# Row transfers between HBM and SBUF cut into four groups of 32 partitions instead of two halves of 128

## The chip, the cores and the metric

The kernel runs on one core of a Trainium2 chip. The metric is the device time of one execution in microseconds (us). The kernel before takes 1252.09 us (median of 2 runs, 1251.47 to 1252.70).

## The reference, cut to what matters

Forward and backward pass of one transformer block on x of 2048 rows by 512 columns, bfloat16. The attention is local and dilated: with 32 heads of 16 columns, row s looks at the rows s, s-2, ..., s-14. The block is followed by a GELU feed-forward layer of 1792 columns. Outputs are the block's result (out_0), the gradient of x (out_1) and those of the six weights and biases.

```python
H = 32; W, dil = 8, 2
idx = pos[:, None] - (jnp.arange(W) * dil)[None, :]
logits = jnp.einsum("bhsd,bhswd->bhsw", q, k[idx]) * Dh ** -0.5   # masked where idx < 0
o = jnp.einsum("bhsw,bhswd->bhsd", _softmax(logits), v[idx])
h = x + o @ wo                                  # x @ wqkv on _layernorm(x) gave q, k, v
out = h + (_gelu(_layernorm(h) @ w1 + b1) @ w2 + b2)
_out, _vjp = jax.vjp(_f, A_x, A_wqkv, A_wo, B_w1, B_b1, B_w2, B_b2)
```

## The kernel before

The 2048 rows are worked on in four chunks (c = 0 to 3). A chunk does not hold 512 neighbouring rows: 32 places of 64 rows each are formed (`TPR` = 64, `PR` = 32), and chunk c takes 16 neighbouring rows out of each place. A tile of a chunk, [128, 4, 512], holds them so: partition 32 n + p, for n = 0 to 3, has of place p the rows 2n, 2n+1 of the first eight and the same two of the last eight. So a chunk is moved between such a tile and a plain array in HBM by an access pattern of three dimensions: 4 (the n), 32 (the p), two rows in a piece.

Three helpers do this. `put_rows` (L152) writes a tile to HBM and `get_rows` (L156) reads one, each in two halves of 128 partitions through `half_rows` (L147), whose outermost dimension is `Q4` = 4. `row4` (L226) reads whole rows for the weighted sums: a tile of 128 partitions by 10 rows of 1 KB, in two pieces of five rows; here too the outermost dimension on the HBM side is 4, since the four groups of 32 partitions start one window step apart. `feat4` (L248) and `att4` (L238) read parts of rows, and already in four groups of 32 partitions.

```python
return _ap(ap2d, [[2 * n, Q4], [TPR * n, PR], [1, 2 * n]], off=(pad + CJ * c + HJ * f) * n)   # half_rows
in_=_ap(d_t[:, :], [[abs(shift) * n, Q4], [TPR * n, PR], [1, nn * n]], off=(t0 + j0) * n)     # row4
```

The program has these stages; times are of the profiled execution.

- Forward, 0 to about 430 us. `f_qkv` (L290) normalises a chunk, forms q, k and v with TensorE, copies them from PSUM to SBUF with ScalarE (`qkv`, L304) and writes them with `put_rows` from POOL to `k_r`, `q_r`, `v_r`. `f_attn` (L307) reads parts of rows back (`k`, `q`), forms logits and softmax and writes the weights (`at_r`). `f_o` (L331) reads rows of `v_r` with `row4` and sums them (`wsum`, L272: VectorE multiplies at L279, TensorE adds up at L285). `f_h` adds x, read anew with `get_rows`. `f_ffn` (L362) is the feed-forward layer; it writes out_0 in halves from the ACT queue (L397).
- First part of backward, about 430 to 690 us: the feed-forward layer's gradients. `gout` is read with `get_rows` from POOL (L459). Here TensorE is busy nearly all the time.
- Second part of backward, about 690 to 1185 us: attention. `b_go` (L591) writes `go_r` with `put_rows`; `b_ga` (L603) reads `bv` and `go` with `feat4`, VectorE multiplies (L262), and `gl_r` is written; `b_sum` (L620) runs three times per chunk (sel 2, 0, 1), each time with two `row4` tiles `r` (of `go_r`, `k_r`, `q_r`; pool tag `w4`, three buffers) and eight multiplications at L279; `b_gx` (L641) forms the gradient of x (`ln_bwd`, last step `gx`, L489) and writes out_1 in halves from POOL (L657). In between, `weights_gen` (L665) puts in the products for the weights' gradients, with tiles `h1tm` of 1 MB.
- Last, to 1247 us: the gradient of wqkv (L734) from tiles read again.

The order on each engine is made by the tile scheduler that builds the program: it lists the instructions of each queue by its own estimate of when they can start, and each queue then runs in that order. DMAs are issued by SP (`sync`), ACT and POOL (`pq`); a queue's next DMA waits behind one whose data are not ready. Each DMA has one of eight completion semaphores of its kind (one set for SP and ACT, one for POOL), used in turn, so that a ninth DMA waits for the first.

Of the kernel before, what the change touches and what calls it, by code (L numbers as in the profile page):

```python
# [10 lines left out]
P = 128  # L11
BF16 = mybir.dt.bfloat16
# [14 lines left out]
Q4 = 4  # L27
PR = P // Q4


def _ap(a, dims, off=0):
    return bass.AP(tensor=a.tensor, offset=a.offset + off, ap=[list(d) for d in dims])
# [3 lines left out]
def kernel(  # L36
# [20 lines left out]
    nc = tc.nc  # L57
    xf = A_x.flatten_outer_dims()
    gof = grad_out.flatten_outer_dims()
    out0f = out_0.flatten_outer_dims()  # L60
# [83 lines left out]
    def pv(d_t):  # L144
        return d_t[:, :].rearrange("p (t d) -> p t d", t=TC)

    def half_rows(ap2d, c, f, pad=0):  # L147

        n = ap2d.shape[-1]
        return _ap(ap2d, [[2 * n, Q4], [TPR * n, PR], [1, 2 * n]], off=(pad + CJ * c + HJ * f) * n)  # L150

    def put_rows(eng, ap2d, c, t_, pad=0):  # L152
        for f in range(2):
            eng.dma_start(out=half_rows(ap2d, c, f, pad), in_=t_[:, 2 * f:2 * f + 2, :].rearrange("p i d -> p (i d)"))

    def get_rows(eng, t_, ap2d, c):  # L156
        for f in range(2):
            eng.dma_start(out=t_[:, 2 * f:2 * f + 2, :].rearrange("p i d -> p (i d)"), in_=half_rows(ap2d, c, f))


    fl = pool("fl", 1)
# [64 lines left out]
    def row4(pool_, d_t, t0, nj, name, tag, bufs, shift):  # L226


        n = d_t.shape[-1]
        t_ = pool_.tile([P, nj, n], BF16, name=name, tag=tag, bufs=bufs)  # L230
        t0 += min(0, shift) * (Q4 - 1)
        for j0 in range(0, nj, 5):
            nn = min(5, nj - j0)
            sync.dma_start(out=t_[:, j0:j0 + nn, :],  # L234
                           in_=_ap(d_t[:, :], [[abs(shift) * n, Q4], [TPR * n, PR], [1, nn * n]], off=(t0 + j0) * n))
        return t_

    def att4(pool_, d_t, t0, nj, name, tag, bufs, shift):  # L238
# [123 lines left out]
    def f_ffn(c):  # L362
        h, ln2T = hs[c], l2T[c]
        gs = []
        for f2 in range(FT // 2):
            u = fl.tile([P, 2, CH], BF16, name=f"u{c}_{f2}", tag="u", bufs=3)
            for i in range(2):
                ft = 2 * f2 + i
                ps = acc(f"psf{c}_{ft}", "accB")
                for dc in range(DC):  # L370
                    nc.tensor.matmul(ps[:], lhsT=w1[:, dc, ft * P:(ft + 1) * P], rhs=ln2T[:, dc, :],  # L371
                                     start=(dc == 0), stop=(dc == DC - 1))
                nc.scalar.activation(out=u[:, i, :], in_=ps[:], func=ACT.Identity, bias=b1c[:, ft:ft + 1], scale=1.0)  # L373
            z = fl.tile([P, 2, CH], BF16, name=f"z{c}_{f2}", tag="z", bufs=2)
            nc.vector.tensor_tensor(out=z[:], in0=u[:], in1=u[:], op=ALU.mult)
            nc.vector.tensor_scalar(out=z[:], in0=z[:], scalar1=GK, scalar2=1.0, op0=ALU.mult, op1=ALU.add)
            nc.vector.tensor_tensor(out=z[:], in0=z[:], in1=u[:], op=ALU.mult)
            s = fl.tile([P, 2, CH], BF16, name=f"s{c}_{f2}", tag="s", bufs=2)
            nc.scalar.activation(out=s[:], in_=z[:], func=ACT.Sigmoid, scale=2.0 * GC)
            gt = fl.tile([P, 2, CH], BF16, name=f"g{c}_{f2}", tag="g", bufs=7)  # L380
            nc.vector.tensor_tensor(out=gt[:], in0=u[:], in1=s[:], op=ALU.mult)
            gs.append(gt)
            r0, r1 = 2 * f2 * P, (2 * f2 + 2) * P
            for dd, t_ in ((x_d[c][r0:r1, :], u), (s_d[c][r0:r1, :], s), (g_d[r0:r1, c * CH:(c + 1) * CH], gt)):
                pq.dma_start(out=dd.rearrange("(i p) t -> p i t", p=P), in_=t_[:])
        for j in range(TC):
            ps = acc(f"ps2{c}_{j}", "accB")
            for ft in range(FT):
                nc.tensor.matmul(ps[:], lhsT=gs[ft // 2][:, ft % 2, j * P:(j + 1) * P], rhs=w2[:, ft, :],  # L389
                                 start=(ft == 0), stop=False)  # L390
            nc.tensor.matmul(ps[:], lhsT=ones_row[:], rhs=b2row[:], start=False, stop=False)
            nc.tensor.matmul(ps[:], lhsT=ident[:], rhs=h[:, j, :], start=False, stop=True)
            if j % 2 == 0:
                o0 = fl.tile([P, 2, D], BF16, name=f"o0{c}_{j}", tag="o0", bufs=2)
            nc.scalar.copy(out=o0[:, j % 2, :], in_=ps[:])
            if j % 2 == 1:
                nc.scalar.dma_start(out=half_rows(out0f, c, j // 2), in_=o0[:].rearrange("p i d -> p (i d)"))  # L397

    def f_wT(src, ns, dst, nb):
        n2 = 8 // ns if ns <= 8 else 1  # L400
# [76 lines left out]
    def ln_bwd(ps, xhat, r, resid, out_ap, nm):  # L477
        s2 = const.tile([P, 2], F32, name=f"s2{nm}", tag="s2", bufs=4)
        junk = bl.tile([P, D], BF16, name=f"jk{nm}", tag="junk", bufs=2)
        nc.scalar.activation(out=junk[:], in_=ps, func=ACT.Identity, accum_out=s2[:, 0:1])  # L480
        junk2 = bl.tile([P, D], BF16, name=f"jl{nm}", tag="junk", bufs=2)
        nc.vector.tensor_tensor_reduce(out=junk2[:], in0=ps, in1=xhat, scale=1.0, scalar=0.0,
                                       op0=ALU.mult, op1=ALU.add, accum_out=s2[:, 1:2])
        c2 = const.tile([P, 2], F32, name=f"c2{nm}", tag="c2", bufs=4)
        nc.vector.tensor_scalar(out=c2[:], in0=s2[:], scalar1=r, scalar2=-1.0 / D, op0=ALU.mult, op1=ALU.mult)
        u = bl.tile([P, D], F32, name=f"lu{nm}", tag="lu", bufs=2)
        nc.scalar.activation(out=u[:], in_=xhat, func=ACT.Identity, bias=c2[:, 0:1], scale=c2[:, 1:2])
        nc.vector.scalar_tensor_tensor(out=u[:], in0=ps, scalar=r, in1=u[:], op0=ALU.mult, op1=ALU.add)  # L488
        nc.vector.tensor_tensor(out=out_ap, in0=u[:], in1=resid, op=ALU.add)  # L489
# [151 lines left out]
    def b_gx(c):  # L641
        ln1 = bp.tile([P, TC, D], BF16, name=f"bln1{c}", tag="bln1", bufs=1)
        pq.dma_start(out=ln1[:], in_=pv(ln1_d[c]))
        for j in range(TC):
            ps = acc(f"psy{c}_{j}", "gx", 2)
            n = 0
            for sel in (2, 0, 1):
                for g in range(G):
                    nc.tensor.matmul(ps[:], lhsT=gts[c, sel][:, g, j * P:(j + 1) * P], rhs=wqkvT[:, sel * G + g, :],  # L649
                                     start=(n == 0), stop=(n == NJ - 1))  # L650
                    n += 1
            t = c * TC + j
            if j % 2 == 0:
                gx = bp.tile([P, 2, D], BF16, name=f"gx{t}", tag="gx", bufs=2)
            ln_bwd(ps[:], ln1[:, j, :], rstd1[:, t:t + 1], gh[c][:, j, :], gx[:, j % 2, :], f"a{t}")
            if j % 2 == 1:
                pq.dma_start(out=half_rows(out1f, c, j // 2), in_=gx[:].rearrange("p i d -> p (i d)"))  # L657

    br1.release()
    bp = pool("bp", 1, side="right")  # L660
# [111 lines left out]
```

## Time and profile before

| what | us |
|---|---|
| median of 2 runs | 1252.09 (1251.47 to 1252.70) |
| the profiled execution | 1248.67 |
| its span, first to last instruction | 1246.9 |
| busy in the span: TensorE, VectorE, ScalarE, POOL | 756.1, 560.1, 436.6, 331.8 |
| mean granted clock of TensorE | 0.795 of full |

An engine's busy time is the sum over its instructions. A wait is put down to the instruction or DMA that came last before the waiting engine could go on. The chain is followed back from the last instruction, at each step to what released it. The DMA share is the mean busy share of the 16 DMA engines.

### The profile page before, as it was taken

To read this page: it belongs to the slowest core of one execution; us is meant where nothing else is said; L and a number is where in the kernel's file an instruction comes from. 1 tells how busy PE (TensorE), PEld (TensorE's weight loads), DVE (VectorE), ACT (ScalarE), POOL (GpSimd) and SP (SyncE) were. 2 spreads that over 40 slices of the span, in tenths; PEclk is the share of its full clock that TensorE was granted. 3 is DMA by queue.
4 is the path that set the end of the run, shared out by engine and by line. 5 is a ranking of instruction groups with operands and counts; after the bars stand their busy time and mean duration, and the time that the engine had idled before them with its cause. 6 is when DMAs were issued, how large, how long until landed. Compare 5 with 4: busy or idle time off the path is not lost.

```text
span 1246.9 us, 11658 instructions
## 1 busy us (share of the span) xinstructions
PE 756.1 (61%) x4306; PEld 343.9 (28%) x4306; DVE 560.1 (45%) x879; ACT 436.6 (35%) x600; POOL 331.8 (27%) x474
## 2 busy tenths in 40 slices
PE   1664515656558859999998626443445354454558
PEld 0322102322223324444454314120113122121123
DVE  3210355660855544888763034618346253253400
ACT  2333203543344545878775301020220221121201
POOL 3333222442242744443220323132032111100020
PEclk9887756687879989999999859575667776787669
DMA  6555434465354896666552776463365554433071
GB/s 200 157 131 141 113 72 125 156 195 157 108 187 154 273 279 200 191 186 180 174 154 89 194 154 148 133 158 104 117 174 147 148 157 138 139 131 124 30 291 38
DMA packets 72006, 191.54 MB, mean 154 GB/s; under 512 B 19821, under 2 KB 27854, under 8 KB 71950
## 3 DMA queue, kind: packets, MB, share of 16 engines
q0 software_dynamic: 49920, 128.67, 37.2%
q1 hardware_dynamic: 12892, 54.27, 12.5%
q10 hardware_dynamic: 9138, 7.87, 2.1%
q8 instruction: 33, 0.54, 0.2%
q14 instruction: 23, 0.19, 0.1%
HBM read 122.43 MB, written 68.24 MB: 153 GB/s over the span
## 4 chain that ended last, share of the span: by engine, by line
DMA 34%; issue 20%; PE 19%; DVE 11%; POOL 7%; ACT 5%; another core or an unknown queue 2%; SPq 2%; ACTq 0%; POOLq 0%; DVEq 0%
DMA r<-go_r 6%; DMA h1tm<-h1tm_d 4%; DMA k_r<-qkv 4%; PE psq L734 4%; DMA r<-q_r 3%; DMA r<-k_r 2%; DVE pb L279 2%; PE psw L677 2%; PE ps L389 2%; DMA s_d<-s 2%; DMA gout<-in_grad_out_dram 2%; SPq L234 2%; DMA w1T_d<-wT 2%; PE psw L509 1%
## 5 line engine op out<-in xcount | busy, mean ns | idle before, releaser
L279 DVE TENSOR_TENSOR pb<-ba,r 128x2048 bf16<-128x2048 bf16 x96 | 113.4, 1220 | 149.1 <-DMA r<-go_r 68.4
L285 PE MATMUL pss<-pb,sel 128*32 128x512 bf16 x384 | 48.1, 497 | 123.6 <-DVE pb L279 122.9
L262 DVE TENSOR_TENSOR pag<-go,bv 128x4096 bf16<-128x4096 bf16 x16 | 36.3, 2288 | 121.0 <-DMA go<-go_r 98.1
L649 PE MATMUL psy<-wqkvT,gT 128*128 128x512 bf16 x192 | 65.4, 491 | 29.4 <-ACT gT L224 18.9
L302 PE MATMUL psq<-wqkv,ln1T 128*128 128x512 bf16 x192 | 59.2, 466 | 39.2 <-ACT qkv L304 38.3
L371 PE MATMUL psf<-ln2T,w 128*128 128x512 bf16 x224 | 66.2, 441 | 25.1 <-ACT u L373 25.1
L677 PE MATMUL psw<-h1tm,ln2a 128*128 128x256 bf16 x448 | 65.7, 298 | 24.7 <-DMA h1tm<-h1tm_d 22.1
L637 ACT ACTIVATE gt<-pss 128x512 bf16<-128x512 f32 x32 | 19.0, 598 | 143.2 <-PE pss L285 141.7
L262 DVE TENSOR_TENSOR pa<-q,k 128x4096 bf16<-128x4096 bf16 x16 | 36.3, 2287 | 69.9 <-DMA k_r<-qkv 48.5
L285 PEld LDWEIGHTS <-sel 128*32 128x32 bf16 x512 | 15.2, 97 | 182.6 <-issue 100.4
L389 PE MATMUL ps<-w,g 128*128 128x512 bf16 x224 | 56.7, 400 | 3.9 <-ACT u L373 3.1
L544 PE MATMUL psg<-goutT,w2T 128*128 128x512 bf16 x224 | 58.0, 379 | 0.1
L677 PEld LDWEIGHTS <-ln2a 128*128 128x128 bf16 x448 | 44.2, 105 | 46.1 <-issue 21.0
L734 PE MATMUL psq<-gqa,ln1a 128*128 128x512 bf16 x192 | 44.1, 395 | 19.3 <-DMA gqa<-gq_d 19.3
L509 PE MATMUL psw<-gout,gtm 128*128 128x512 bf16 x224 | 53.0, 379 | 0.0
L565 PE MATMUL psx<-w1T,gh 128*128 128x512 bf16 x224 | 52.1, 379 | 1.2 <-DVE luf L488 1.1
L304 ACT CAST qkv<-psq 128x512 bf16<-128x512 f32 x48 | 27.2, 588 | 62.9 <-DMA k_r<-qkv 34.6
L279 DVE TENSOR_TENSOR pbo<-a,v 128x2048 bf16<-128x2048 bf16 x32 | 38.0, 1216 | 22.7 <-PE pso L285 21.1
L268 PE MATMUL ga<-pag,sel 128*32 128x512 bf16 x128 | 17.3, 562 | 48.9 <-DVE pag L262 48.9
L638 POOL DMA_DIRECT2D gq_d<-gt x12 | 6.9, 575 | 146.9 <-ACT gt L637 79.5
L373 ACT ACTIVATE u<-psf,b1c 128x512 bf16<-128x512 f32 x56 | 36.8, 686 | 21.3 <-DMA x_d<-u 10.9
L546 DVE CUSTOM_DVE_ANT_0 gh<-psg,by 128x512 bf16<-128x512 f32 x56 | 37.6, 687 | 13.6 <-PE psg L544 12.7
(191 smaller groups left out, 1573.9 us busy)
## 6 DMA issues: line engine op xcount, KB each, us to landing
v<-v_r SPq DMA_DIRECT2D x16, 640.0 KB
r<-go_r SPq DMA_DIRECT2D x16, 640.0 KB
r<-k_r SPq DMA_DIRECT2D x16, 640.0 KB
r<-q_r SPq DMA_DIRECT2D x16, 640.0 KB
x_d<-u POOLq DMA_DIRECT2D x28, 256.0 KB, 4.6
s_d<-s POOLq DMA_DIRECT2D x28, 256.0 KB, 4.1
g_d<-g POOLq DMA_DIRECT2D x28, 256.0 KB, 4.7
bu<-x_d POOLq DMA_DIRECT2D x28, 256.0 KB, 3.6
```

Source lines behind the costliest of these rows:

```text
L262: nc.vector.tensor_tensor(out=pr[:], in0=_ap(q_ap, [q_ap.ap[0], [P, 4], [0, W], [1, P]]), in1=_ap(k_ap, [k_ap.ap[0], [P, 4], [-DIL * P, W] ...
L279: nc.vector.tensor_tensor(out=pr[:].rearrange("p n (d h) -> p n d h", h=H), in0=_ap(a_ap, [a_ap.ap[0], [4 * H, 4], [0, DH], [1, H]], off=w ...
L285: nc.tensor.matmul(ps[PR * n:PR * n + PR, :], lhsT=sel4[:], rhs=prs[wh][:, n, :], start=(wh == 0), stop=(wh == 1))
L302: nc.tensor.matmul(ps[:], lhsT=ln1T[:, dc, j * P:(j + 1) * P], rhs=wqkv[:, dc, sel * D:(sel + 1) * D], start=(dc == 0), stop=(dc == DC - 1))
L371: nc.tensor.matmul(ps[:], lhsT=w1[:, dc, ft * P:(ft + 1) * P], rhs=ln2T[:, dc, :], start=(dc == 0), stop=(dc == DC - 1))
L389: nc.tensor.matmul(ps[:], lhsT=gs[ft // 2][:, ft % 2, j * P:(j + 1) * P], rhs=w2[:, ft, :], start=(ft == 0), stop=False)
L509: nc.tensor.matmul(ps[:], lhsT=gtm[:, t, :], rhs=gout[t // TC][:, t % TC, :], start=(t == 0), stop=(t == NT - 1))
L544: nc.tensor.matmul(ps[:], lhsT=w2T[:, dc, ft * P:(ft + 1) * P], rhs=gT[:, dc, :], start=(dc == 0), stop=(dc == DC - 1))
L565: nc.tensor.matmul(ps[:], lhsT=gh1[ft // 2][:, ft % 2, j * P:(j + 1) * P], rhs=w1T[:, ft, :], start=(ft == 0), stop=(ft == FT - 1))
L649: nc.tensor.matmul(ps[:], lhsT=gts[c, sel][:, g, j * P:(j + 1) * P], rhs=wqkvT[:, sel * G + g, :], start=(n == 0), stop=(n == NJ - 1))
L677: nc.tensor.matmul(ps[:, i * 2 * P:(i + 1) * 2 * P], lhsT=ln2a[:, t // TC, t % TC, dc * P:(dc + 1) * P], rhs=tmx[:, t, :], start=(t == 0), ...
L734: nc.tensor.matmul(ps[:], lhsT=ln1a[:, t // TC, t % TC, dc * P:(dc + 1) * P], rhs=gqt[:, t // TC, t % TC, :], start=(t == NT - 1), stop=(t ...
```

## The change

`half_rows` goes. `rows` describes one group n of 32 partitions: 32 places outermost, then the two pairs of rows. `put_rows` and `get_rows` issue four such DMAs for a tile (256 KB halves become 128 KB quarters for a [128, 4, 512] tile) where there were two. `row4` issues four DMAs, one for each group of 32 partitions with all its 10 rows, where there were two of 128 partitions by five rows. out_0 and out_1 are now gathered in a tile of the whole chunk with one buffer (before: two buffers of half a chunk) and written at the chunk's end with `put_rows` from SP; before, out_0 was written from ACT and out_1 from POOL.

```diff
-        return _ap(ap2d, [[2 * n, Q4], [TPR * n, PR], [1, 2 * n]], off=(pad + CJ * c + HJ * f) * n)
+    def rows(ap2d, c, n, pad=0):
+        m = ap2d.shape[-1]
+        return _ap(ap2d, [[TPR * m, PR], [HJ * m, 2], [1, 2 * m]], off=(pad + CJ * c + 2 * n) * m)
+
+    def quarter(t_, n):
+        return t_[PR * n:PR * n + PR, :, :].rearrange("p (f i) d -> p f (i d)", f=2)
 
     def put_rows(eng, ap2d, c, t_, pad=0):
-        for f in range(2):
-            eng.dma_start(out=half_rows(ap2d, c, f, pad), in_=t_[:, 2 * f:2 * f + 2, :].rearrange("p i d -> p (i d)"))
+        for n in range(Q4):
+            eng.dma_start(out=rows(ap2d, c, n, pad), in_=quarter(t_, n))
...
@@ row4
-        for j0 in range(0, nj, 5):
-            nn = min(5, nj - j0)
-            sync.dma_start(out=t_[:, j0:j0 + nn, :],
-                           in_=_ap(d_t[:, :], [[abs(shift) * n, Q4], [TPR * n, PR], [1, nn * n]], off=(t0 + j0) * n))
+        for s_ in range(Q4):
+            sync.dma_start(out=t_[PR * s_:PR * s_ + PR, :, :].rearrange("p (a b) d -> p a (b d)", a=2),
+                           in_=_ap(d_t[:, :], [[TPR * n, PR], [nj // 2 * n, 2], [1, nj // 2 * n]], off=(t0 + abs(shift) * s_) * n))
@@ f_ffn
-            if j % 2 == 0:
-                o0 = fl.tile([P, 2, D], BF16, name=f"o0{c}_{j}", tag="o0", bufs=2)
-            nc.scalar.copy(out=o0[:, j % 2, :], in_=ps[:])
-            if j % 2 == 1:
-                nc.scalar.dma_start(out=half_rows(out0f, c, j // 2), in_=o0[:].rearrange("p i d -> p (i d)"))
+            if j == 0:
+                o0 = fl.tile([P, TC, D], BF16, name=f"o0{c}", tag="o0", bufs=1)
+            nc.scalar.copy(out=o0[:, j, :], in_=ps[:])
+        put_rows(sync, out0f, c, o0)
@@ b_gx
-            if j % 2 == 0:
-                gx = bp.tile([P, 2, D], BF16, name=f"gx{t}", tag="gx", bufs=2)
-            ln_bwd(ps[:], ln1[:, j, :], rstd1[:, t:t + 1], gh[c][:, j, :], gx[:, j % 2, :], f"a{t}")
-            if j % 2 == 1:
-                pq.dma_start(out=half_rows(out1f, c, j // 2), in_=gx[:].rearrange("p i d -> p (i d)"))
+            if j == 0:
+                gx = bp.tile([P, TC, D], BF16, name=f"gx{t}", tag="gx", bufs=1)
+            ln_bwd(ps[:], ln1[:, j, :], rstd1[:, t:t + 1], gh[c][:, j, :], gx[:, j, :], f"a{t}")
+        put_rows(sync, out1f, c, gx)
```

The scheduler's order changes with it. First place: SP's queue in the second part of backward, around the end of chunk 0. In `r_210` the first digit is sel, the second the chunk and the third the half of the chunk; `gx_6071` is chunk 0's whole gradient. Before, the row loads follow one another:

```order
L234 DMA r_101_5866<-q_r 128x1x2560 x2
L234 DMA r_210_6101<-go_r 128x1x2560 x2
L234 DMA r_211_6132<-go_r 128x1x2560 x2
L234 DMA r_010_6227<-k_r 128x1x2560 x2
L234 DMA r_011_6258<-k_r 128x1x2560 x2
L234 DMA r_110_6422<-q_r 128x1x2560 x2
```

In the changed kernel the four writes of out_1 stand among them:

```order
L236 DMA r_101_5966<-q_r 32x5120 x4
L236 DMA r_210_6204<-go_r 32x5120 x4
L236 DMA r_211_6237<-go_r 32x5120 x4
L236 DMA r_010_6334<-k_r 32x5120 x3
L157 DMA out_dram<-gx_6071 32x2x1024 x4
L236 DMA r_010_6334<-k_r 32x5120
L236 DMA r_011_6367<-k_r 32x5120 x4
```

The last quarter of `r_010` and all row loads behind it now stand behind a DMA that needs the last `gx` of chunk 0. For chunks 1 and 2 the same stands in front of the last quarter of `r_221` and of `r_231`.

Second place: VectorE's queue at the end of chunk 1, in the changed kernel. `gx_6673` is chunk 1's gradient, `pb` are the multiplications at L279 (L281 in the changed file).

```order
L281 TENSOR_TENSOR pb_11_6828<-ba_2_6799,r_220_6806 128x2048
L489 SCALAR_TENSOR_TENSOR lua_6729<-psy_2_6709,rstd_80,lua_6729 128x512
L486 TENSOR_SCALAR c2a_6751<-s2a_6746,rstd_80 128x2
L490 TENSOR_TENSOR gx_6673<-lua_6729,gh_2958 128x512
L489 SCALAR_TENSOR_TENSOR lua_6753<-psy_3_6733,rstd_80,lua_6753 128x512
L490 TENSOR_TENSOR gx_6673<-lua_6753,gh_2958 128x512
L281 TENSOR_TENSOR pb_20_6845<-ba_2_6799,r_221_6839 128x2048
```

The last `gx` of chunk 1 now stands directly ahead of the first multiplication that reads `r_221`; before, multiplications of two more `r` tiles were mixed in among the `gx` steps.

Third place: POOL's queue at the start of the second part of backward, in the changed kernel. `go_5161`, `go_5254` and `go_5409` are the tiles of chunks 0, 1 and 2 that go to `go_r` or, for `go_0`, come back from it.

```order
L157 DMA go_r<-go_5161 32x2x1024 x4
L668 DMA ln2a<-ln_d_100 128x2048
L668 DMA ln2a<-ln_d_101 128x2048
L668 DMA ln2a<-ln_d_102 128x2048
L671 DMA h1tm_5195<-h1tm_d 128x16x256
L157 DMA go_r<-go_5254 32x2x1024 x4
L254 DMA bv_0_5283<-v_r 32x30x128 x4
L254 DMA go_0_5288<-go_r 32x16x128 x4
L157 DMA go_r<-go_5409 32x2x1024 x4
```

Each write of a `go` tile is four DMAs in a row now; the order of the tiles is that of before.

## Rows read from the trace of the kernel before

**Rows 1.** Busy time by stretch; PE, DVE, ACT, POOL, granted clock, DMA share, GB/s.
```profile
50.00:150.00 100.00, 54.83 (x254) 23.59 (x254) 16.61 (x31) 32.34 (x51) 26.07 (x36) 0.78 0.51 135
420.00:490.00 70.00, 54.88 (x230) 21.55 (x228) 28.33 (x48) 31.55 (x41) 36.01 (x51) 0.88 0.87 259
690.00:1200.00 510.00, 240.95 (x1485) 109.93 (x1483) 201.69 (x224) 94.45 (x154) 95.67 (x140) 0.70 0.50 142
```

**Rows 2.** Waits from 700 to 1190 us: engine, line, releaser: total, times, longest.
```profile
POOL out_dram L657 <- DVE gx L489: 103.2, 8, 31.6
DVE pag L262 <- DMA go<-go_r: 98.1, 4, 41.8
...
DVE pb L279 <- DMA r<-go_r: 68.4, 6, 16.1
...
DVE pb L279 <- DMA r<-q_r: 39.6, 4, 12.2
DVE pb L279 <- DMA r<-k_r: 35.9, 5, 10.5
...
DVE pag L262 <- PE ga L268: 22.8, 4, 12.4
```

**Rows 3.** Busy time by short stretches, columns as in rows 1.
```profile
638.40:640.00 1.60, 1.59 (x8) 0.70 (x8) 0.49 (x1) 1.60 (x3) 0.19 (x1) 1.00 1.02 392
...
890.00:900.00 10.00, 5.44 (x22) 1.89 (x23) 8.04 (x13) 2.10 (x3) 0.00 (x0) 0.50 0.25 103
997.00:1007.00 10.00, 6.34 (x33) 2.59 (x34) 7.37 (x12) 2.70 (x4) 1.00 (x2) 0.52 0.25 104
...
1094.00:1104.00 10.00, 6.66 (x30) 2.21 (x30) 7.37 (x12) 1.30 (x2) 0.00 (x0) 0.59 0.25 104
...
1190.00:1198.50 8.50, 0.00 (x0) 0.10 (x1) 0.00 (x0) 0.00 (x0) 2.29 (x5) 0.50 1.00 390
```

**Rows 4.** Issues of the row loads on SP: ns min/median/max, first and last start.
```profile
L234 SPq DMA_DIRECT2D r<-go_r x16: 507/3859/15601, 704.9 to 1054.2; - x16
...
L234 SPq DMA_DIRECT2D r<-q_r x16: 507/6316/14984, 777.7 to 1115.8; - x16
```

**Rows 5.** Chain that ended last, second part of backward: start, us, what.
```profile
887.76 30.46 DMA r<-k_r
...
1054.18 41.76 DMA r<-go_r
```

**Rows 6.** DMA issues: destination and source, queue, count, KB each, median us to landing.
```profile
x_d<-u POOLq DMA_DIRECT2D x28, 256.0 KB, 4.6
...
k_r<-qkv POOLq DMA_DIRECT2D x8, 256.0 KB, 9.3
...
q<-q_r POOLq DMA_DIRECT2D x16, 128.0 KB, 7.3
...
gout<-in_grad_out_dram POOLq DMA_DIRECT2D x8, 256.0 KB, 16.9
...
go<-go_r POOLq DMA_DIRECT2D x16, 128.0 KB, 13.1
```

**Rows 7.** Chain that ended last, forward: start, us, what.
```profile
1.51 9.97 DMA x<-in_A_x_dram
...
45.23 10.00 DMA k_r<-qkv
...
134.01 9.73 DMA k_r<-qkv
...
432.62 20.66 DMA gout<-in_grad_out_dram
```

**Rows 8.** Issues on POOL: ns min/median/max, first and last start.
```profile
L154 POOL DMA_DIRECT2D k_r<-qkv x8: 708/730/752, 41.6 to 134.0; - x8
...
L252 POOL DMA_DIRECT2D q<-q_r x16: 649/668/736, 121.4 to 306.4; - x16
...
L252 POOL DMA_DIRECT2D go<-go_r x16: 653/663/679, 705.6 to 926.4; - x16
```

**Rows 9.** Part 1 of the page: busy us, share of the span, instructions.
```profile
PE 756.1 (61%) x4306; PEld 343.9 (28%) x4306; DVE 560.1 (45%) x879; ACT 436.6 (35%) x600; POOL 331.8 (27%) x474
```

More of the change, by code (lines that the diff above doesn't have):

```diff
@@ L145, in pv @@
         return d_t[:, :].rearrange("p (t d) -> p t d", t=TC)
-    def half_rows(ap2d, c, f, pad=0):
-        n = ap2d.shape[-1]
-        return _ap(ap2d, [[2 * n, Q4], [TPR * n, PR], [1, 2 * n]], off=(pad + CJ * c + HJ * f) * n)
+    def rows(ap2d, c, n, pad=0):
[3 more added lines that the diff above has]
+        return t_[PR * n:PR * n + PR, :, :].rearrange("p (f i) d -> p f (i d)", f=2)
     def put_rows(eng, ap2d, c, t_, pad=0):
-        for f in range(2):
-            eng.dma_start(out=half_rows(ap2d, c, f, pad), in_=t_[:, 2 * f:2 * f + 2, :].rearrange("p i d -> p (i d)"))
+        for n in range(Q4):
+            eng.dma_start(out=rows(ap2d, c, n, pad), in_=quarter(t_, n))
     def get_rows(eng, t_, ap2d, c):
-        for f in range(2):
-            eng.dma_start(out=t_[:, 2 * f:2 * f + 2, :].rearrange("p i d -> p (i d)"), in_=half_rows(ap2d, c, f))
+        for n in range(Q4):
+            eng.dma_start(out=quarter(t_, n), in_=rows(ap2d, c, n))
     fl = pool("fl", 1)
```

## The prediction

> **What bounds the kernel now.** I first read busy time by stretch, to see which stage has slack. From 690 to 1200 us VectorE is busy for 201.69 of 510 us and TensorE for 240.95, at a granted clock of 0.70 [rows 1]. No engine is near its limit there, so the stage waits for something. Then the waits of that stage: VectorE stands still for 68.4 + 39.6 + 35.9 = 143.9 us until a row tile `r` has landed, and for 98.1 us until `go` has [rows 2]. These 242 us are most of its 308 idle ones. Then the chain: four pieces "DMA r" of 30 to 42 us each lie on it, the first at 887.76 and the last at 1054.18, 146.5 us together [rows 5].
>
> Why are the row loads late? A tile is 128 x 10 rows x 1 KB = 1.31 MB. In three stretches in which almost nothing but row loads moves, the DMA share is 0.25 and the rate 103 to 104 GB/s, while loads of 128-partition tiles reach a share of 1.00 and 390 GB/s [rows 3]. A quarter of 16 engines is four, and the outermost dimension of these transfers is four. The stretch at 638.40 speaks for the shape and against the queue: it holds a load `gr` from the same SP queue, 128 partitions outermost, and has a share of 1.02 (of two queues together) [rows 3]. So a row tile takes 1.31 MB / 104 GB/s = 12.6 us, and the 24 tiles of the second part of backward need 302 us of the roughly 411 us between the first issue at 704.9 and the last at 1115.8 [rows 4], before any sharing with other transfers. That queue is what bounds the stage. Its issues show the same: at best 0.507 us, at median 3.9 to 6.3, at worst over 15 [rows 4]; SP is held up because what it issued before has not drained.
>
> The other transfers with an outermost 4 behave alike: 256 KB of `k_r` written from POOL takes 9.3 us to land, 256 KB of `x_d` with 128 partitions outermost 4.6 [rows 6].
>
> **The change part by part.** The sum is against the profiled execution, 1248.67 us; the median of the runs is 3.4 above it, which I add at the end.
>
> 1. Row loads. With 32 outermost I expect all 16 engines: 1.31 MB at 390 GB/s is 3.4 us per tile, 24 tiles 81 us, hidden under 240 us of TensorE work, since three buffers let loads run ahead. That removes the 143.9 us. Two things come back. First, SP's queue: in the changed order the four writes of out_1 stand before the last quarter of `r_010`, `r_221` and `r_231`, and wait for a chunk's last `gx`. VectorE's next instruction, or the next but one, needs that quarter. After the last `gx` come four issues of 0.5 us [rows 4] and a landing; the nearest rows for one are 4.6 us (`x_d`) and 7.3 us (`q`, also 32 partitions) [rows 6]. I take 6, so 8 us, three times: 24. Second, VectorE will then wait for TensorE more than now, since `r` no longer comes last; the nearest row is its present wait for `ga`, 22.8 us [rows 2], and I add as much again: 23. Net -144 + 24 + 23 = -97. Bounds: -144 if nothing comes back; at the other end POOL's present wait for `gx`, 103.2 us in two waits for each of four chunks [rows 2], moves to SP and is exposed in full for the three chunks that have row loads behind it, 77 us: -144 + 77 + 23 = -44. I take the value near the better end, because one landing is what stands between `gx` and the next multiplication.
>
> [...]
>
> 2. Loads of `go`. They already have 32 outermost, but land in 13.1 us against 7.3 for `q`, the same shape at another time [rows 6]. Four of the engines are busy with rows in that stage, and a transfer spread over all ends with its slowest; and `go_r` is written with 4 outermost. Four waits by 5.8 us would be -23. Against it, each `go` tile is now written by four DMAs in a row ahead of other work on POOL. I take -5; bounds -23 and +6 (eight more issues of 0.7 us [rows 8]).
>
> 3. Writes of q, k and v in the forward stage. From 45 to 144 us five pieces of the chain are landings of `k_r` or `v_r`, the first and the last 10.00 and 9.73 us [rows 7]; TensorE is busy for 55 of 100 us there [rows 1]. At 4.6 instead of 9.3 us [rows 6] each saves 4.7: -23. A tile's first half now waits for its second and is issued with it, as four issues of about 0.66 us instead of two of 0.73 [rows 8]: +1 us each, +5. I take -18; bounds -23 and +10 (two more casts and issues at each of five places).
>
> 4. The first load of x, on the chain with 9.97 us [rows 7]: 512 KB at 104 GB/s are 5.0 us, at 390 are 1.3: -4; bounds -5 and 0.
>
> 5. `gout`: 16.9 us to land [rows 6], on the chain with 20.66 [rows 7]. But DMA share is 0.87 there already [rows 1], so spreading helps little: -4; bounds -12 and 0.
>
> 6. out_0 from SP instead of ACT, out_1 from SP instead of POOL. POOL loses eight issues and its waits for `gx`; behind the last of them stand the loads of the last stage, 0.7 us: -1. out_0 stands in front of loads that are not due for tens of us: 0.
>
> 7. POOL's count: 24 tiles with two more issues, `gout` eight more, out_1 eight fewer: 48 more by 0.66 us [rows 8] are 32 us on an engine that is busy for 27% [rows 9]. What is on the path is in 2 and 3; for the rest +3, bounds 0 and +32. The cover is POOL's idle time; if that goes, the 32 are due.
>
> Sum: -97 - 5 - 18 - 4 - 4 - 1 + 3 = -126. 1248.67 - 126 = 1122.7, and 3.4 more for the median: 1126 us.
>
> **The rivals.**
>
> A. SP takes over the wait for `gx`. For it: the order, with row loads behind out_1 in three chunks, and 103.2 us of waits for `gx` [rows 2]. Against it: two row tiles, or nearly so, are still loaded ahead. Row loads gain 44 instead of 97: 1126 + 53 = 1179 us.
>
> B. The row loads only look like the bound, and `go`'s chain (written to HBM, read back, multiplied) or TensorE takes their place in full. For it: the 98.1 us wait for `go` [rows 2], which the change touches little. Against it: the last `go` load is issued at 926.4 [rows 8], and the longest "DMA r" piece, 41.76 us, comes after that [rows 5]. Step 1 gives nothing, the others hold: 1126 + 97 = 1223 us, within 2% of before, or just beyond.
>
> C. Slower: SP's row loads keep to 104 GB/s whatever their shape, because the pace is that of long pieces and not of four engines. For it: all stretches at that rate are row loads [rows 3]. Against it: the `gr` stretch, though it has POOL's transfers in it too. Then a row tile still takes 12.6 us, and the saturated queue gets out_1 as well: four tiles of 0.52 MB, 5 us each, 20 us, and it stands still three times for `gx`, 24 us. The forward gains of 3 to 5 fall away, and POOL's 5 and 3 us remain: 1248.67 + 20 + 24 + 8 = 1301, with the median 1304 us. This decides if a row load that runs alone still shows a DMA share of 0.25.
>
> **How the numbers follow.** My forecast has 0.80, A 0.11, B 0.05 and C 0.04. The likeliest case's own range is 1065 to 1185: at the low end step 1 keeps most of its 144 us and `go` its 23; at the high end step 1 falls to -44 and nearly all else is as summed. The range of 8 in 10 takes in A and stops short of B: 1060 to 1200. A change of 2% is 25 us, about what a measurement of this kernel can tell from no change; 2% faster is 1227. Forecast and A are faster: 0.91. B is split about its edge, but I count it as no change: 0.05. C is slower: 0.04.
>
> **What would show it.** Step 1 is right if VectorE's waits for `r` fall from 143.9 us to under 50, if the DMA share in a stretch with row loads alone is well over 0.25, and if SP's issues of row loads come down to about 0.5 us at median. The price of the new wait is seen on SP, in its wait for `gx` ahead of out_1, and on VectorE right after each chunk's last `gx`. Step 2 is right if `go` lands in under 10 us, step 3 if `k_r` lands in about 5 and the attention after it begins some 18 us earlier. The forecast is wrong if 690 to 1200 shrinks by less than 60 us: with a share still at 0.25, C is the cause; with `r` on time and `go` or TensorE in its place, B; with SP waiting long for `gx` and `r` late behind it, A.

## The result and the profile after

The kernel after takes 1088.84 us (median of 2 runs, 1088.37 to 1089.31) against 1252.09: a ratio of 0.8696, 95% interval 0.8659 to 0.8734. It is 163 us faster; 126 were forecast. The time lies in the range given (1060 to 1200). The profiled execution took 1088.37 us, span 1086.6.

Three rows bound the stages: the first matmul of the feed-forward layer (`psf`), the last one of the weight gradient in the first part of backward (`psw`), and the first one of the last stage (`psq`, line L734). Their first and last start are the two numbers behind the durations. Of the kernel before:

```profile
L371 PE MATMUL psf<-ln2T,w x224: 376/379/634, 216.9 to 467.1; 128*128 128x512 bf16 x112
L509 PE MATMUL psw<-gout,gtm x224: 379/379/390, 507.0 to 678.8; 128*128 128x512 bf16 x112
L734 PE MATMUL psq<-gqa,ln1a x192: 379/379/634, 1199.4 to 1243.1; 128*128 128x512 bf16 x192
```

and of the kernel after:

```profile
L373 PE MATMUL psf<-ln2T,w x224: 376/379/634, 192.8 to 413.6; 128*128 128x512 bf16 x112
L510 PE MATMUL psw<-gout,gtm x224: 376/379/390, 443.6 to 628.6; 128*128 128x512 bf16 x112
L734 PE MATMUL psq<-gqa,ln1a x192: 379/379/634, 1039.0 to 1082.8; 128*128 128x512 bf16 x192
```

So three stages got shorter. Up to the feed-forward layer: 216.9 to 192.8, 24 us (forecast 22, steps 3 and 4). From there to the end of the first part of backward: 461.9 to 435.8, 26 us (forecast about 1: the 4 of `gout`, less the 3 of POOL's issues). Second part of backward: 520.6 to 410.4, 110 us (forecast 103). The last stage is as it was. The surprise is the 26.

Below, busy time by stretch, with the columns of [rows 1]: the second part of backward, then two short stretches with row loads alone.

```profile
690.00:1040.00 350.00, 204.06 (x1327) 96.83 (x1326) 190.91 (x216) 88.77 (x142) 81.20 (x125) 0.74 0.70 172
...
973.30:979.60 6.30, 2.07 (x13) 0.55 (x14) 4.42 (x4) 0.59 (x1) 0.00 (x0) 0.50 1.01 224
979.00:985.50 6.50, 4.42 (x27) 2.27 (x24) 5.09 (x5) 2.61 (x3) 0.56 (x1) 0.50 1.01 222
```

Against [rows 3] a row load alone went from a share of 0.25 and 104 GB/s to a share of 1.01 and 222 to 224 GB/s. All 16 engines are busy, as forecast, but the rate is not the 390 GB/s that step 1 took.

The waits of the second part of backward, in the columns of [rows 2]:

```profile
DVE pag L264 <- DMA go_r<-go: 45.9, 1, 45.9
...
DVE pag L264 <- DMA go<-go_r: 32.4, 2, 19.6
...
DVE pb L281 <- DMA r<-k_r: 20.3, 5, 7.2
...
DVE pb L281 <- DMA r<-go_r: 7.9, 1, 7.9
DVE pb L281 <- DMA r<-q_r: 7.8, 3, 4.7
```

VectorE's wait for `r` fell from 143.9 to 36.0 us; its wait for `go` or for a write of it only from 98.1 to 78.3. The wait of 45.9 us is the first of the stage, and the multiplication behind it reads chunk 0's `go`, whose last load was issued at 657.7 us and took 17.2 to land; the write of chunk 2's `go` that the wait is put down to landed at about the same moment. Before, the same first wait was 41.8 us.

A new wait came in place of some of the old. VectorE's step `jla` of `ln_bwd` (a sum over the gradient that TensorE has formed) is held up until ScalarE's step `jka` on the same gradient, here before and after:

```profile
DVE jla L482 <- ACT jka L480: 12.2, 4, 7.6
DVE jla L483 <- ACT jka L481: 45.9, 9, 19.3
```

SP now waits for `gx` ahead of out_1 (the waits of SP's queue):

```profile
SPq L157 <- DVE gx L490: 109.1, 4, 39.5
```

The other signs that the prediction named, in the columns of [rows 4] and [rows 6]:

```profile
L236 SPq DMA_DIRECT2D r<-go_r x32: 302/364/897, 641.6 to 969.8; - x32
```

```profile
go<-go_r POOLq DMA_DIRECT2D x16, 128.0 KB, 11.9
```

SP's issues came down as forecast. `k_r` lands in 2.7 us, and attention's first multiplication starts at 111.2 us in place of 136.6. But `go` lands in 11.9 us, not in under 10.

### The profile page after: what moved, and what is told of

Read it like the earlier page. It is cut to its first block, busy times and chain, and to the rows that moved or that the text cites. A ratio compares the mean times of both kernels' runs of the same rounds, so it can differ in the third digit from the quotient of the medians.

```text
span 1086.6 us, 11848 instructions
## 1 busy us (share of the span) xinstructions
PE 735.2 (68%) x4306; PEld 343.2 (32%) x4306; DVE 557.5 (51%) x879; ACT 438.5 (40%) x600; POOL 347.3 (32%) x522
## 4 chain that ended last, share of the span: by engine, by line
PE 30%; DMA 15%; DVE 14%; ACT 7%; issue 7%; POOL 4%; SPq 0%; DVEq 0%; ACTq 0%; POOLq 0%
DMA h1tm<-h1tm_d 5%; PE psq L734 4%; PE ps L391 4%; PE psy L650 4%; PE psw L677 3%; DVE pb L281 3%; PE psw L510 2%; PE psg L545 2%; PE psx L566 2%; DVE pag L264 1%; DMA r<-q_r 1%; DMA x_d<-u 1%; DMA go<-go_r 1%; PE psf L373 1%; PE pswo L691 1%
## 5 line engine op out<-in xcount | busy, mean ns | idle before, releaser
L281 DVE TENSOR_TENSOR pb<-ba,r 128x2048 bf16<-128x2048 bf16 x96 | 112.0, 1218 | 41.0 <-DMA r<-k_r 20.3
L264 DVE TENSOR_TENSOR pag<-go,bv 128x4096 bf16<-128x4096 bf16 x16 | 36.2, 2286 | 101.2 <-DMA go_r<-go 45.9
L650 PE MATMUL psy<-wqkvT,gT 128*128 128x512 bf16 x192 | 61.7, 481 | 9.3 <-DVE lua L489 9.2
L287 PE MATMUL pss<-pb,sel 128*32 128x512 bf16 x384 | 42.4, 451 | 31.7 <-DVE pb L281 31.6
L304 PE MATMUL psq<-wqkv,ln1T 128*128 128x512 bf16 x192 | 52.7, 427 | 5.5 <-ACT qkv L306 5.1
L734 PE MATMUL psq<-gqa,ln1a 128*128 128x512 bf16 x192 | 44.2, 395 | 15.8 <-DMA gqa<-gq_d 15.8
L680 ACT CAST ow<-psw 128x512 bf16<-128x512 f32 x14 | 8.2, 586 | 112.3 <-PE psw L677 112.3
L281 DVE TENSOR_TENSOR pbo<-a,v 128x2048 bf16<-128x2048 bf16 x32 | 37.8, 1211 | 19.9 <-PE pso L287 19.9
L225 PE MATMUL ptq<-ident,gt 128*128 128x128 bf16 x192 | 26.5, 269 | 28.4 <-ACT gt L638 12.8
L270 PEld LDWEIGHTS <-sel 128*32 128x32 bf16 x256 | 9.7, 114 | 111.5 <-issue 86.7
L377 DVE TENSOR_TENSOR z<-u 128x1024 bf16<-128x1024 bf16 x28 | 19.2, 687 | 41.8 <-ACT u L375 41.6
```

The costliest lines, as they stand in the source:

```text
L264: nc.vector.tensor_tensor(out=pr[:], in0=_ap(q_ap, [q_ap.ap[0], [P, 4], [0, W], [1, P]]), in1=_ap(k_ap, [k_ap.ap[0], [P, 4], [-DIL * P, W] ...
L281: nc.vector.tensor_tensor(out=pr[:].rearrange("p n (d h) -> p n d h", h=H), in0=_ap(a_ap, [a_ap.ap[0], [4 * H, 4], [0, DH], [1, H]], off=w ...
L287: nc.tensor.matmul(ps[PR * n:PR * n + PR, :], lhsT=sel4[:], rhs=prs[wh][:, n, :], start=(wh == 0), stop=(wh == 1))
L304: nc.tensor.matmul(ps[:], lhsT=ln1T[:, dc, j * P:(j + 1) * P], rhs=wqkv[:, dc, sel * D:(sel + 1) * D], start=(dc == 0), stop=(dc == DC - 1))
L734: nc.tensor.matmul(ps[:], lhsT=ln1a[:, t // TC, t % TC, dc * P:(dc + 1) * P], rhs=gqt[:, t // TC, t % TC, :], start=(t == NT - 1), stop=(t ...
```

## The experiments

Runs that change the kernel before answer to its 1252.09 us, runs that change the kernel after to its 1088.84. The ratio is always to the kernel before.

**Row loads alone, in the kernel before.**

```diff
-        for j0 in range(0, nj, 5):
-            nn = min(5, nj - j0)
-            sync.dma_start(out=t_[:, j0:j0 + nn, :], in_=...[[abs(shift) * n, Q4], [TPR * n, PR], [1, nn * n]]...)
+        for s_ in range(Q4):
+            sync.dma_start(out=t_[PR * s_:PR * s_ + PR, :, :]..., in_=...[[TPR * n, PR], [nj // 2 * n, 2], [1, nj // 2 * n]]...)
```

> The kernel before with the row loads alone in groups of 32 partitions. Theory (the outermost 4 held the row loads to 104 GB/s, and that bounded the second part of backward): the stage from the last psw to the last stage falls from 520.6 us by 90 to 110 us, the forward part stays within 6 us of before, the total is about 1252 - 100 = 1150 us; VectorE's wait for r falls from 143.9 us to under 50. Rival (the gain needs the written rows too, since go_r, q_r and k_r are written in outermost 4 just ahead of their loads): the stage falls by less than 60 us, total over 1190 us.

Measured: 1119.54 us, ratio 0.8924 (0.8881 to 0.8967), 30 us more gain than expected. The same three rows:

```profile
L370 PE MATMUL psf<-ln2T,w x216: 376/379/634, 209.5 to 439.3; 128*128 128x512 bf16 x108
L508 PE MATMUL psw<-gout,gtm x217: 379/379/390, 478.7 to 650.4; 128*128 128x512 bf16 x109
L733 PE MATMUL psq<-gqa,ln1a x188: 379/379/631, 1072.2 to 1116.0; 128*128 128x512 bf16 x188
```

The second part of backward falls by 98.8 us to 421.8, so the written rows are not needed for that. VectorE's waits there:

```profile
DVE jla L481 <- ACT jka L479: 49.6, 9, 21.2
...
DVE pb L278 <- DMA r<-q_r: 7.3, 3, 3.6
```

Its wait for `r` is 137 us shorter than before, and the stage only 99. So 38 us came back, about as much as the wait for `jka` grew (12.2 before).

But 7 us go ahead of the feed-forward layer, and 21 more between there and the first part's end (461.9 to 440.9). `row4` is also called in the forward stage, for eight tiles of `v_r` (`f_o`, L335), and the prediction counted only the 24 of backward.

**The eight v tiles alone, in the kernel before.** The same edit in a copy of `row4` that only `f_o` calls.

```diff
-            v4 = row4(fr, v_r, PAD + CJ * c + HJ * f - 2, HJ + 2, f"v4_{c}{f}", "w4", 2, -4)
+            v4 = row4q(fr, v_r, PAD + CJ * c + HJ * f - 2, HJ + 2, f"v4_{c}{f}", "w4", 2, -4)
```

> The kernel before with the eight v tiles of the forward stage alone in groups of 32 partitions, a part of step 1 that the prediction did not count. Theory (the v loads held four engines while small transfers of attention and FFN waited): the start of FFN comes about 7 us earlier, the stage from 217 to 484 us is about 21 us shorter, the second part of backward stays at 521, total about 1225 us. Rival (those 28 us of the run with all row loads changed came from elsewhere, such as the clock): total within 8 us of before.

Measured: 1224.81 us, ratio 0.9783 (0.9740 to 0.9825): 27 us. Its rows:

```profile
L380 PE MATMUL psf<-ln2T,w x216: 376/379/635, 206.6 to 441.8; 128*128 128x512 bf16 x108
L518 PE MATMUL psw<-gout,gtm x217: 379/379/390, 481.8 to 653.4; 128*128 128x512 bf16 x109
L743 PE MATMUL psq<-gqa,ln1a x188: 379/379/631, 1173.0 to 1216.1; 128*128 128x512 bf16 x188
```

The feed-forward layer begins 10 us earlier, the stretch from there to 653.4 is 15 us shorter (446.8), the second part of backward is the same (519.6). So 15 of the 26 us that step 5 did not hold are the v tiles', and 10 more of theirs lie ahead of it. Which waits they come off is not known.

**Loads of `gout` alone, in the kernel before.** They were my first suspect for those 26 us, since `gout` lands in 4.5 us now and in 16.9 before [rows 6].

```diff
-        get_rows(pq, gout[c], gof, c)
+        get_quarters(pq, gout[c], gof, c)
```

> The kernel before with only the loads of gout in groups of 32 partitions, one part of step 5, which was put at 4 us. Theory (the unforecast 30 us between 217 and 484 us are gout's, whose pieces sat 16.9 us on four engines and held POOL's queue and the activations behind it): total 20 to 30 us under before, about 1227 us, and gout lands in about 5 us. Rival (the 30 us come from the written rows, at_r above all, or from out_0's move to SP): total within 8 us of before.

Measured: 1244.28 us, ratio 0.9947 (0.9921 to 0.9973): 3 to 10 us, though `gout` does land in 4.3. At its own place, from the first `psf` to the last `psw`, it is 4 us (457.6 for 461.9). My theory fell; the term of step 5 (4 us) was of the right size.

**Row writes alone, in the kernel before.** `put_rows` as in the change; out_0 and out_1 as before.

```diff
-        for f in range(2):
-            eng.dma_start(out=half_rows(ap2d, c, f, pad), in_=...)
+        for n in range(Q4):
+            eng.dma_start(out=rows(ap2d, c, n, pad), in_=quarter(t_, n))
```

> The kernel before with only the row writes (q, k, v, attn, go, gl) in groups of 32 partitions. Theory (steps 2 and 3 of the prediction, 18 and 5 us): attention begins about 18 us earlier, total 18 to 30 us under before, about 1230 us. Rival for the stage from 217 to 484 us (the 30 us there come from the writes): that stage falls by 20 to 30 us too, total about 1205 us.

Measured: 1241.34 us, ratio 0.9899 (0.9857 to 0.9941): 11 us under 1252.09, 12 under the runs of the kernel before that were taken beside it. The feed-forward layer begins at 215.4, only 1.5 us earlier, and the second part of backward falls by 6. That is half of what steps 2 and 3 gave together, and hardly any of it lies where step 3 put it:

```profile
L378 PE MATMUL psf<-ln2T,w x216: 376/379/634, 215.4 to 467.3; 128*128 128x512 bf16 x108
```

**The writes taken back, in the kernel after.**

```diff
-            put_rows(pq, d_t[:, :], c, t_, pad)
+            put_halves(pq, d_t[:, :], c, t_, pad)
```

(and so for `at_r`, `go_r` and `gl_r`; `put_halves` is the old `put_rows`)

> The kernel after with only POOL's row writes (k, q, v, at, go, gl) back in halves with 4 outermost; writing them in groups of 32 partitions was worth 12 us by itself in the kernel before, where attention did not start earlier. Theory (writes spread over all engines gain only once the row loads no longer fill four of them): the last psq of the forward stage comes 10 to 16 us later than 128.4, go and go_r land later, total about 1110 us. Rival (the writes are worth the same 12 us in both kernels): total about 1100 us, with less than 6 us of it ahead of the last psq.

Measured: 1126.80 us, ratio 0.8997 (0.8952 to 0.9041): 38 us slower than after, 17 more than the theory's total. Its three rows:

```profile
L379 PE MATMUL psf<-ln2T,w x216: 376/379/634, 203.4 to 423.3; 128*128 128x512 bf16 x108
L516 PE MATMUL psw<-gout,gtm x219: 376/379/390, 453.0 to 637.6; 128*128 128x512 bf16 x110
L740 PE MATMUL psq<-gqa,ln1a x188: 379/379/631, 1085.3 to 1129.3; 128*128 128x512 bf16 x188
```

The first `psf` starts at 203.4 in place of 192.8, so some 11 us are the forward stage's. The rest is in the second part of backward, 447.7 against 410.4 in the profiled run (1134.86 us, 8 above the median, so 27 to 37 us). VectorE's waits for `go`, `go_r` and `gl_r` are longer there, 106.3 us in place of 78.3:

```profile
DVE pag L270 <- DMA go_r<-go: 48.2, 1, 48.2
DVE pag L270 <- DMA go<-go_r: 39.0, 2, 25.5
...
DVE pag L270 <- DMA ba<-gl_r: 19.1, 1, 19.1
```

The writes are worth 38 us with the row loads fixed and 12 without: the two parts of the change help each other, as they would if a transfer that is spread over all engines still ended with the four that row loads fill. That mechanism fits both runs; it was not isolated further, and a different order of the queues is not ruled out.

**The outermost dimension back to 4, in groups of 32 partitions.**

```diff
-            ... [[TPR * n, PR], [nj // 2 * n, 2], [1, nj // 2 * n]] ...
+            ... [[TPR * n, 4], [4 * TPR * n, 8], [1, nj * n]] ...
```

> The kernel after, with each row load still a group of 32 partitions, but its rows read in the order 0, 4, 8, ... so that the outermost dimension is 4 again and the next 8, with all 10 rows as one piece; the rows land on other partitions than the sums want, with the same bytes. Theory (the outermost dimension sets the number of engines): a row load alone is back to about 104 GB/s and a share of 0.25, the second part of backward is back to about 500 us, total about 1190 us. Rival (it is the group of 32 partitions, or four transfers in flight in place of two, that gives the rate): over 200 GB/s, total within 10 us of 1089.

Measured: 1240.38 us, ratio 0.9897 (0.9867 to 0.9927). The second part of backward is at 523.8, so all that it had gained is lost. The total is 50 us over the expected one. 35 of them lie ahead of the second part, in stages that are 13 and 22 us longer than in the kernel after and whose only row loads are the v tiles; the expectation left these out too. Two stretches with row loads alone:

```profile
1094.00:1104.00 10.00, 3.06 (x21) 1.03 (x22) 4.63 (x4) 1.17 (x2) 0.14 (x1) 0.50 0.25 108
1112.00:1122.00 10.00, 2.66 (x18) 0.73 (x17) 3.57 (x4) 1.20 (x2) 0.00 (x0) 0.57 0.25 107
```

A share of 0.25 again, 107 to 108 GB/s, with 32 partitions and four transfers a tile. The pieces are of 10 KB here and in the kernel after, since a sequence's ten rows lie one behind the other; in the trace of the kernel after, 141 packets of rows move 1.44 MB from 979.0 to 985.5 us. So here the outermost dimension, 4 or 32, decides between a share of 0.25 and one of 1.0, and the groups of 32 do not.

**The other way round: 32 outermost, all 128 partitions in a transfer.**

```diff
+        for j0 in range(0, nj, 5):
+            nn = min(5, nj - j0)
+            sync.dma_start(out=t_[:, j0:j0 + nn, :], in_=...[[TPR * n, PR], [abs(shift) * n, Q4], [1, nn * n]]...)
```

> The kernel after, with each row tile loaded by two transfers over 128 partitions as before (five rows each), but with the 32 sequences of the layout outermost and the 4 shifts second; the rows land on other partitions than the sums want, with the same bytes. [...] Rival 1 (what helps is the groups of 32): back to 104 GB/s, total about 1230. [...]

Measured: 1007.25 us, ratio 0.8038 (0.8003 to 0.8072), 82 us under after, far more than the 4 to 24 that I had expected (a total of 1065 to 1085 us). In its order on SP, out_1's writes stand behind all row tiles of the next chunk, so two things changed at once. The following runs part them.

**out_1 put off, in the kernel after.**

```diff
-        put_rows(sync, out1f, c, gx)
+        gxs[c] = gx
...
+        if c > 0:
+            put_rows(sync, out1f, c - 1, gxs[c - 1])
         take(wg, 1)
         b_gx(c)
```

> The kernel after, with each chunk's write of out_1 put off on SP until the next chunk's go and k sums have been issued, so that SP waits for no gx ahead of row loads that are due. Theory (the wait for gx on SP costs the 24 us that the prediction gave it): the second part of backward falls from 410 to about 390 us, total about 1067. Rival (the late tiles are bounded by VectorE and buffers, SP's wait lies beside them): total within 6 us of 1089; the wait for r stays near 36 us.

Measured: 1069.50 us, ratio 0.8540 (0.8500 to 0.8579): 19 us less. The second part of backward is 390.9 us:

```profile
L510 PE MATMUL psw<-gout,gtm x219: 376/379/390, 446.0 to 631.0; 128*128 128x512 bf16 x110
L739 PE MATMUL psq<-gqa,ln1a x188: 379/379/631, 1021.9 to 1064.5; 128*128 128x512 bf16 x188
```

VectorE's wait for `r` falls from 36.0 to 4.1, and 19 of these 32 us reach the time. The price of 24 us that step 1 gave to SP's wait for `gx` was nearly right.

**The order of the four transfers.** `for s_ in (0, 2, 1, 3)` in place of `range(Q4)`.

> The kernel after, with the four transfers of a row tile issued in the order 0, 2, 1, 3. [...] Rival (transfers of one queue follow one another on each engine, so the order changes nothing): about 220 GB/s still, total within 5 us of 1089.

Measured: 1088.58 us, ratio 0.8692 (0.8639 to 0.8745): no difference in time. The rate alone goes from 222 to 259 GB/s:

```profile
968.00:976.00 8.00, 2.98 (x20) 0.95 (x21) 5.58 (x5) 1.17 (x2) 0.05 (x1) 0.50 1.03 259
```

My estimate had been more than 300, and 1075 to 1087 us in all. What takes the rate from 222 to 259 no run shows.

**128 partitions with nothing left out.** In the run with all 128 partitions the rows no longer met their weights. Here the weights of the sums are loaded onto the same partitions, and a second selection matrix adds neighbours.

```diff
-               in_=...[[TPR * n, PR], [nj // 2 * n, 2], [1, nj // 2 * n]]...
+               in_=...[[TPR * n, PR], [abs(shift) * n, Q4], [1, nn * n]]...     # row4, 128 partitions, five rows
-            pq.dma_start(out=t_[PR * s_:PR * s_ + PR, :, :],
+            pq.dma_start(out=t_[:, :, :].rearrange("(r s) j n -> s r j n", s=Q4)[s_],
+        nc.vector.tensor_reduce(out=selw[:], in_=_ap(ident[:], [ident[:].ap[0], [Q4, PR], [1, Q4]]), axis=AX.X, op=ALU.add)
-                nc.tensor.matmul(ps[PR * n:PR * n + PR, :], lhsT=sel4[:], ...
+                nc.tensor.matmul(ps[PR * n:PR * n + PR, :], lhsT=selw[:], ...
```

> A version meant to beat both kernels: the row tile loaded by two transfers over 128 partitions with the 32 sequences outermost, as in the run that put rows on other partitions, but here the weights ba and a4 are loaded onto the same partitions (4 r + s in place of 32 s + r) and a second selection matrix sums neighbouring partitions, so nothing is left out. Theory (the 7 per cent under the kernel after come from the rate of the row loads and the later place of out_1's writes on SP, not from what the values were): total 1000 to 1015 us. Rival (weights written to every fourth partition land later and take it back): over 1030 us.

Measured: 1001.32 us, ratio 0.7999 (0.7967 to 0.8030), 88 us under after. The second part of backward:

```profile
L514 PE MATMUL psw<-gout,gtm x219: 376/379/390, 438.7 to 623.8; 128*128 128x512 bf16 x110
L738 PE MATMUL psq<-gqa,ln1a x188: 379/379/634, 951.5 to 995.6; 128*128 128x512 bf16 x188
```

It is 327.7 us, 63 under that of the run with out_1 put off; in the scheduler's order out_1's writes stand behind the next chunk's row tiles here too. The two differ in more than the partitions that a transfer reaches: pieces are of 5 KB instead of 10, a tile has two transfers instead of four, and the weights lie elsewhere. A stretch with row loads, by busy time and by queue (SP's is q1: packets, MB, share of 16 engines):

```profile
878.00:884.00 6.00, 5.90 (x41) 2.57 (x41) 2.06 (x2) 2.76 (x5) 3.20 (x5) 1.00 1.03 400
```

```profile
q1 hardware_dynamic: 490, 2.24, 92.7%
```

2.24 MB in 6 us are 373 GB/s of rows. The share is about the same 1.0 as at 222 GB/s in the kernel after.

**The same, cut at partition 64.**

```diff
+        for h_ in range(2):
...
+                sync.dma_start(out=t_[2 * PR * h_:2 * PR * h_ + 2 * PR, j0:j0 + nn, :],
+                               in_=...[[TPR * n, PR // 2], [abs(shift) * n, Q4], [1, nn * n]]...)
```

> The version that loads a row tile over 128 partitions, with the same bytes, pieces of five rows, weights and sums, and out_1's writes put off so that SP's order stays the same; but each of a tile's two transfers is cut into the partitions 0 to 63 and 64 to 127, with 16 sequences outermost, and the lower half goes first. [...] Rival (220 GB/s came from the groups of 32, from pieces of 10 KB or from four transfers per tile): rows alone well over 300 GB/s, total 1000 to 1015 us.

Measured: 1036.35 us, ratio 0.8255 (0.8217 to 0.8292), between the 1000 to 1015 us of the rival and the 1055 to 1075 that I had expected, as with groups of 32 and out_1 put off. The rate alone is within the 220 to 250 GB/s that I had expected, and not the rival's well over 300:

```profile
796.00:802.00 6.00, 5.39 (x38) 2.18 (x36) 5.02 (x9) 2.40 (x6) 0.25 (x1) 0.93 1.03 227
...
941.00:947.00 6.00, 4.06 (x19) 2.24 (x20) 3.08 (x3) 2.59 (x3) 0.54 (x1) 0.50 1.04 222
```

With 64 partitions at a time, twice as many as in a group of 32, and the same pieces as at 400 GB/s, rows move at 222 to 227. Transfers are half as large as there, but the next run has 64 partitions with transfers of the same 640 KB, and the rate stays. So the limit goes with which partitions a transfer reaches: 222 to 229 GB/s on 32 or 64 of them (259 on 32 in the order 0, 2, 1, 3), 373 on all 128. Why that is so, no run shows. But the time is 33 us below the run of groups of 32 with the same order on SP.

**Halves with pieces of 10 KB.**

```diff
-                               in_=...[[TPR * n, PR // 2], [abs(shift) * n, Q4], [1, nn * n]]...
+                           in_=...[[TPR * n, PR // 2], [abs(shift) * n, Q4], [1, nj * n]]...
```

> The same halves of 64 partitions, with all 10 rows of a sequence as one piece of 10 KB in place of two of 5 KB, so two transfers per tile in place of four. It asks why halves took 1036 us where groups of 32, at the same 220 GB/s alone, took 1069 with the same order on SP. Theory (a small transfer such as go waits on each engine behind pieces of 10 KB, twice as long as behind 5 KB): go lands in 11 to 13 us again in place of 8.9, total 1055 to 1075 us. Rival (it is the 64 partitions, or the weights on every fourth partition): go under 10 us, total 1030 to 1042 us.

Measured: 1058.02 us, ratio 0.8431 (0.8389 to 0.8474). Row loads alone, by busy time and by queue:

```profile
930.00:936.00 6.00, 5.64 (x25) 2.44 (x24) 4.50 (x11) 3.18 (x7) 0.00 (x0) 0.93 1.00 229
```

```profile
q1 hardware_dynamic: 166, 1.37, 99.6%
```

The rate is the same as with 5 KB, but the time is 22 of the 33 us longer. So these go with the pieces, or with transfers of twice the size; the two were not parted. The loads of `go` move the way of the theory, though less than it had, here by landing (last number) with pieces of 10 KB, then of 5 KB:

```profile
go<-go_r POOLq DMA_DIRECT2D x16, 128.0 KB, 10.8
```

```profile
go<-go_r POOLq DMA_DIRECT2D x16, 128.0 KB, 8.9
```

With groups of 32 and 10 KB it is 11.9. The other 11 us (partitions 0 to 63 instead of 32, two transfers a tile instead of four, or the weights' places) stay open.

## Why the prediction was right, and where its terms were off

The sign, the place and the main mechanism held: an outermost 4 kept the row loads to a share of 0.25, four of 16 engines, as the run with 4 outermost and 32 partitions shows best. Rival C (row loads keep to 104 GB/s) is refuted by the 222 of the kernel after. Rival A (SP's wait for `gx` exposed) had the right place, but cost 19 us and not 77. Rival B (`go` takes the place of the rows in full) falls with the 98.8 us of the row loads alone; `go` is now the largest wait of VectorE, but not in place of theirs. That the total came within 37 us is partly luck, because errors offset each other. Term by term:

- Step 1, rows of backward: -97 forecast, about -80 measured, as -99 (row loads alone) and +19 (out_1 on SP). Its premise of 390 GB/s failed; 222 was enough to free most of the 143.9 us. What comes back as a wait for other engines was 38 us with the row loads alone, not 23, and it came mainly at ScalarE's `jka` behind the gradient's sums, not at `ga` (22.8 before, 15.7 after).
- Step 1, count: here the forecast failed. "24 tiles" left out the eight v tiles of the forward stage, worth 27 us. I had read the issues of `r` only, and the v tiles go by the same `row4` under another name.
- Step 2, `go`: -5 forecast, and with `gl` some -27 to -37 by the run that took the writes back. I weighed the landing of the load, which hardly moved (13.1 to 11.9 us), mentioned the write of `go_r` without a price and left `gl_r`'s out. The bounds (-23 to +6) did not hold it. In VectorE's waits 28 us of it are seen, 19 of them as a wait for weights read from `gl_r`; but such a wait of 20 us stands in the version with all 128 partitions too, where the writes are spread, so which of it the writes cause is not shown.
- Step 3, q, k and v: -18 forecast, at most -11 measured (the writes of `at_r` are in it), and only with the row loads changed too; alone it was -1.5, though `k_r` landed in 4.2 us.
- Step 4, first x: -4 forecast; the first `psq` starts at 26.8 in place of 32.0, -5.
- Step 5, `gout`: -4 forecast, -3 to -10 measured.
- Steps 6 and 7 (-1 and +3) were not tried by themselves.

Measured, these add up to -80 - 27 - 32 - 11 - 5 - 7 = -162 (with the middle of 27 and 37 for step 2), against the 163 found. The terms were not all measured in the same kernel, so that they close to 1 us is partly luck.

Step 1 took 390 GB/s for the row loads, and 222 had a price of its own. From the run with out_1 put off to the version with all 128 partitions it is 68 us in three steps: 11 for halves of 64 partitions, 22 for pieces of 5 KB, and 35 for all 128 partitions at once (1036.35 - 1001.32; 32 items outermost instead of 16 and two transfers instead of four come with it). Only the last is a change of rate, from 222 or 227 GB/s to 373.

VectorE's wait for `r` was 4.1 us before these steps and is 4.6 after them, so the gain is not in that wait. Nor is it in its waits for `go`, `go_r` and `gl_r`: `go` lands in 7.2 us instead of 11.9, but these waits went from 78.4 to 85.0. What fell is VectorE's wait for `jka` and, from 19.0 us to none, for TensorE's sums `pss`. TensorE ran faster as well: its granted clock over the second part rose from 0.76 to 0.83 of full, and its busy time fell by 18 us. Here first the run with out_1 put off, then the version with 128 partitions:

```profile
DVE jla L483 <- ACT jka L481: 44.0, 9, 13.8
DVE jla L487 <- ACT jka L485: 15.6, 4, 7.2
...
631.00:1021.90 390.90, 235.24 (x1523) 114.75 (x1539) 204.20 (x225) 103.59 (x163) 98.67 (x152) 0.76 0.74 183
623.80:951.50 327.70, 217.45 (x1522) 106.14 (x1539) 200.87 (x225) 101.38 (x163) 98.41 (x152) 0.83 0.73 218
```

Rows at 222 GB/s hold all engines at a share of 1.0 for 1.7 times as long as at 373, also against what else is to pass. That fits; neither how much of the 63 us it makes nor how much the clock does is shown.

## What to carry to other kernels

Look at the outermost dimension of a transfer's pattern and at the partitions that it reaches as two separate limits, and reorder the layout so that one transfer has many outermost items and all 128 partitions. Here the change that widened the outermost dimension took a row load alone from 104 to 222 GB/s and brought 163 us. The version that reaches all partitions, with shorter pieces and out_1's writes later on SP, moved rows at 373 GB/s and brought another 88, of which 35 are measured for going from 64 partitions to 128. When a helper is changed, count all of its callers, under every name that the trace gives their tiles. When writes and loads share engines, price them together: until the row loads were fixed, the writes were worth a third of what they were afterwards (12 against 38 us). When one wait goes, look for what the engine will wait for next; here 38 of 137 us came back elsewhere.

## What the runs showed that I had not expected

- A DMA share of 1.0 is not a full rate: row loads stand at 1.01 with 222 GB/s (32 partitions), 1.03 with 227 (64) and, with a little else beside them, 1.03 with 400 (128). The share does not tell these apart; the GB/s beside it do.
- An outermost 4 gives the share of 0.25 from SP with 5 KB pieces (104 GB/s) and with 10 KB pieces on 32 partitions (108 GB/s): the length of the pieces hardly matters there. In the whole kernel, halves of 64 partitions with 10 KB instead of 5 KB cost 22 us, at the same rate alone.
- Two parts of a change need not add up: row writes are worth 12 us before the row loads are fixed and 38 after.
